# A planned instruction order: other prices for its engines and transfers, spaced products in the running bank, and four more buffers

## The chip, the cores and the metric

The kernel runs on one core of one Trainium2 chip. The time is that of the device in microseconds (us). Three runs of the kernel before gave 995.69, 995.76 and 1001.08 us; the median is 995.76 us. The profile is of one further execution.

## The reference

Attention over 4 batches, 8 heads, 576 tokens and head size 64, four heads with a local mask and four with a strided one; then, on 2304 tokens of 512 features, a gated unit with 1536 hidden features and a softplus unit with 2048:

```python
scores = np.where(masks[None], scale * q @ k.T, -1e9)      # per batch and head
attn = softmax(scores);  x = (attn @ v) laid out as (2304, 512)
xn = x / np.sqrt(np.mean(x * x, -1) + 1e-6) * rms_g
x = (silu(xn @ w_gate) * (xn @ w_val)) @ w_out
h = x @ w_in
out = (np.maximum(h, 0) + np.log1p(np.exp(-np.abs(h)))) @ w_out2
```

The weights come as 64-bit floats, and the kernel reads their bit patterns.

## The kernel before

**Stages.** Attention comes first: 4 batches of 4 head pairs, each pair cut in two, which makes 32 units, numbered 0 to 31 here. A unit has score products (L442), a softmax on VectorE and ScalarE (L454 to L469), transposes (L486), value products (L510) and a copy into `xs`. The queries and keys of a pair have two buffers for each kind of mask, so loads run at most four pairs ahead. When the first 512 tokens are through, their statistics (L347 to L354), their normalisation (L363) and their first gated products are run among the later units; so too for the next 512. Then comes the gated unit for the first 1024 tokens (side 0) and for the other 1280 (side 1), then the softplus unit for side 0 and side 1. A side has two chunks of 512 tokens; side 1 has an odd chunk of 256 as well.

**Products.** Each 32-bit operand is split into a high and a low half (ScalarE rounds, VectorE or GpSimd subtracts), and three products stand for one (`mm3`, L327). Side 0 of the gated unit multiplies plainly (`plain`, L596). The other sides use seven block products for eight (`quad`, L609): one bank, `a`, keeps a running sum. It takes a product, ScalarE copies it out (L619), and only then may it take the next one; so with every product in `a` after the first. Between two of them stands whatever `fill()` puts there (a call of `drain`): one output product (`out1`, `out2`) of an earlier hidden block out of the list `todo`. A second bank, `f`, is read by an add (`plus`, L623) and started afresh in the next `quad`. The products of the odd chunk stand behind the `quad`.

**Weights.** `decode` (L262) loads 512 KB of 64-bit weights into one of two `raw` tiles, makes 32-bit values on ScalarE (L269) and VectorE (L270 to L275), and writes 256 KB to the DRAM tensor `w_kept`, from which `fetch` (L281) reads them later. In side 1 of the gated unit the weights of the softplus unit are decoded ahead, three blocks for each hidden block (`early2`), through the two `cvt` tiles; a `cvt` tile is free when its write to `w_kept` has landed.

**Order.** The whole program is recorded as nodes (`Program.add`) with an engine, a duration and what they read and write. `emit` (L76) then runs a list schedule with these durations: on each engine the node that is ready and due first; due times come from TensorE's own order. A transfer occupies the queue (SP) for 650 ns and its result is ready 1800 ns + 6 ns per KB later, whatever else is under way. TensorE has two lists, the main one and the side one for what is run among the units (`fill`, L806), and takes the head that can begin earlier; within a list its order is that of the program. The order that comes out is fixed: each engine runs its own queue in order, and the waits are semaphores.

## Time and profile before

| | before |
|---|---|
| median of the runs | 995.76 us |
| the profiled execution | 997.98 us |
| its span | 996.2 us |
| TensorE busy | 913.8 us (92%) |
| VectorE busy | 731.4 us (73%) |
| ScalarE busy | 462.2 us (46%) |
| GpSimd busy | 208.9 us (21%) |

The span is the profiled execution without 1.78 us around it. The busy time of TensorE is modelled and overlaps from one product to the next: 222 products of 512 columns in a stretch of 50 us are a full engine. A row of a wait names the instruction that waited and the one that released it.

### The profile page before, as it was taken

What the parts mean: (1) busy time and instruction counts of PE and PEld (TensorE: products, weight loads), DVE (VectorE), ACT (ScalarE), POOL (GpSimd) and SP (SyncE); (2) the same over time, 40 slices, a digit from 0 to 9 for tenths busy, and PEclk for the clock granted to TensorE, in tenths of its full rate; (3) what the DMA queues carried; (4) which work ended last, traced back from release to release, by engine and by line L of the source; (5) the groups of instructions that cost most, each with busy time, mean ns of one, the idle gap of its engine ahead of it and who ended that gap; (6) DMA issues with size and microseconds to landing.
All of it is one profiled execution on the core that took longest, in us unless ns stands there. A gap on an engine that the chain in (4) does not pass through costs nothing.

```text
span 996.2 us, 14061 instructions
## 1 busy us (share of the span) xinstructions
PE 913.8 (92%) x5244; PEld 756.1 (76%) x5244; DVE 731.4 (73%) x1234; ACT 462.2 (46%) x867; POOL 208.9 (21%) x181
## 2 busy tenths in 40 slices
PE   6667869999999889999999988999998899999998
PEld 5556657888888667887787876888886688888877
DVE  6658638899867878688788888767779666666644
ACT  4557664444434344444444454545555444444430
POOL 2335555000013523323333252000004000000000
PEclk9876789999999989999999999999999999999999
DMA  9996112666640345244544202211220401111002
GB/s 198 240 214 164 49 59 95 215 203 216 191 133 14 101 141 180 86 143 148 183 130 148 64 12 64 64 43 43 64 64 12 137 22 43 43 43 42 22 1 106
DMA packets 42036, 103.12 MB, mean 104 GB/s; under 512 B 5040, under 2 KB 5744, under 8 KB 41968
## 3 DMA queue, kind: packets, MB, share of 16 engines
q1 hardware_dynamic: 41968, 102.23, 35.7%
q8 instruction: 41, 0.67, 0.3%
q14 instruction: 27, 0.22, 0.1%
HBM read 79.66 MB, written 22.54 MB: 103 GB/s over the span
## 4 chain that ended last, share of the span: by engine, by line
PE 67%; DVE 15%; DMA 10%; ACT 4%; issue 3%; POOL 1%; SPq 0%; DVEq 0%; ACTq 0%; POOLq 0%
PE bank L333 64%; DMA raw<-w 3%; DMA w_kept<-cvtx 3%; DVE xs L255 2%; DVE w L255 2%; DMA vb<-v_loc 2%; DVE cvu L272 2%; DVE xs L700 1%; DMA rg_sb<-rms_g 1%; DVE win L255 1%; PE bank L510 1%; PE bank L442 1%; DMA ql<-q_t 1%; DVE cvu L270 1%; DVE wout L255 1%
## 5 line engine op out<-in xcount | busy, mean ns | idle before, releaser
L333 PE MATMUL bank<-ob,win 128*128 128x512 f32 (+1 forms) x1560 | 327.4, 360 | 3.0 <-POOL ob L257 1.8
L333 PEld LDWEIGHTS bank<-ob,win 128*128 128x128 f32 x1560 | 264.4, 191 | 48.4 <-POOL ob L257 2.6
L333 PE MATMUL bank<-tb,win 128*128 128x512 f32 x672 | 178.0, 401 | 28.7 <-ACT gv L619 23.6
L333 PEld LDWEIGHTS bank<-tb,win 128*128 128x128 f32 x672 | 126.9, 192 | 64.1 <-ACT gv L619 30.7
L304 ACT ACTIVATE win<-w 128x512 fp32r<-128x512 f32 (+1 forms) x136 | 83.8, 616 | 93.7 <-DVE w L255 32.1
L718 DVE TENSOR_TENSOR xs<-bank,xs 128x512 f32<-128x512 f32 x126 | 86.3, 686 | 36.3 <-PE bank L333 35.9
L255 DVE TENSOR_TENSOR win<-w,win 128x512 fp32r<-128x512 f32 x112 | 83.6, 746 | 23.2 <-ACT win L304 21.1
L333 PE MATMUL bank<-wout,ghx 128*128 128x512 f32 x304 | 93.8, 389 | 0.2 <-DVE xs L718 0.2
L333 PE MATMUL bank<-gh,wout 128*128 128x512 f32 (+1 forms) x256 | 83.7, 355 | 3.0 <-DVE xs L700 1.7
L333 PE MATMUL bank<-ghx,wout 128*128 128x512 f32 x224 | 84.4, 392 | 1.9 <-DVE gvx L671 1.9
L333 PE MATMUL bank<-wout,gh 128*128 128x512 f32 x272 | 84.2, 390 | 0.7 <-DVE xs L718 0.7
L257 POOL TENSOR_TENSOR win<-w,win 128x512 fp32r<-128x512 f32 x24 | 40.5, 1696 | 164.2 <-ACT win L304 149.2
L700 DVE TENSOR_TENSOR xs<-bank,xs 128x512 f32<-128x512 f32 (+1 forms) x100 | 62.2, 628 | 6.9 <-PE bank L333 6.4
L333 PEld LDWEIGHTS bank<-wout,ghx 128*128 128x128 f32 x304 | 57.0, 188 | 12.5 <-issue 0.6
L333 PEld LDWEIGHTS bank<-wout,gh 128*128 128x128 f32 x272 | 50.5, 188 | 11.6 <-DVE xs L718 1.6
L333 PE MATMUL bank<-wout,glx 128*128 128x512 f32 x152 | 59.2, 389 | 0.0
L255 DVE TENSOR_TENSOR w<-w 128x256 f32<-128x256 f32 x112 | 56.7, 507 | 1.5
L272 DVE SCALAR_TENSOR_TENSOR cvu<-raw,cvu 128x512 uint32<-128x512 uint32 x68 | 56.6, 833 | 1.6
L333 PEld LDWEIGHTS bank<-gh,wout 128*128 128x128 f32 x256 | 46.4, 190 | 12.9 <-DVE xs L700 4.9
L623 DVE TENSOR_TENSOR gv<-bank,gv 128x512 f32<-128x512 f32 x44 | 30.3, 689 | 35.1 <-PE bank L333 19.1
L333 PE MATMUL bank<-wout,gl 128*128 128x512 f32 x136 | 52.9, 389 | 0.0
L333 PEld LDWEIGHTS bank<-ghx,wout 128*128 128x128 f32 x224 | 42.3, 189 | 10.9 <-DVE gvx L671 2.1
(119 smaller groups left out, 1365.9 us busy)
## 6 DMA issues: line engine op xcount, KB each, us to landing
raw<-w SPq DMA_DIRECT2D x68, 512.0 KB, 4.2
w<-w_kept SPq DMA_DIRECT2D x56, 256.0 KB, 2.8
w_kept<-cvtx SPq DMA_DIRECT2D x27, 256.0 KB, 3.9
cvt<-w_kept SPq DMA_DIRECT2D x27, 256.0 KB, 2.7
w_kept<-w SPq DMA_DIRECT2D x24, 256.0 KB, 4.0
out<-xs SPq DMA_DIRECT2D x18, 256.0 KB, 2.0
w_kept<-cvt SPq DMA_DIRECT2D x17, 256.0 KB, 4.0
cvtx<-w_kept SPq DMA_DIRECT2D x17, 256.0 KB, 2.9
```

Source lines behind the costliest of these rows:

```text
L255: dve(n, lambda: getattr(nc.vector, name)(o, x, y), r, w)
L257: pool(n, lambda: getattr(nc.gpsimd, name)(o, x, y), r, w)
L270: dve(512, lambda: nc.vector.tensor_scalar(out=u, in0=t.bitcast(U32), scalar1=0x80000000, scalar2=None, op0=ALU.bitwise_and), [kt], [ku], ...
L272: dve(512, lambda: nc.vector.scalar_tensor_tensor(out=u, in0=wlo, scalar=29, in1=u, op0=ALU.logical_shift_right, op1=ALU.bitwise_or), [kra ...
L304: act(n, lambda: nc.scalar.activation(h, t, AF.Copy), [kt], [reg(0, o + lo, o + hi)])
L333: lambda a=a, b=b, i=i, st=st, mv=mv: nc.tensor.matmul(o, lhsT=st[a], rhs=mv[b], start=(first and i == 0), stop=(last and i == m - 1), ski ...
L442: pr.add("PE", 108 if loc else 81, lambda a=a, h=h: nc.tensor.matmul(sp[64 * h:64 * h + 64, a * nk:(a + 1) * nk], lhsT=qt[:, h, q0 + a * s ...
L510: pr.add("PE", 81, lambda a=a, h=h, o=o, t=t: nc.tensor.matmul(xb[64 * h:64 * h + 64, a * nq:(a + 1) * nq], lhsT=vt[r0:r1, v0 + a, 64 * h: ...
L623: dve(CH, lambda: nc.vector.tensor_add(o[0], y[0], o[0]), [y[1], o[1]], [o[1]])
L700: dve(n, lambda: nc.vector.tensor_add(x, pb, x), [kp, kx], [kx])
L718: dve(DM, lambda: nc.vector.tensor_add(x, pb, x), [kp, kx], [kx])
```

## The change

The planner's prices change: a fixed part of 110 instead of 69 ns for VectorE, 100 ns + n/0.98 instead of 93 ns + n/1.2 for ScalarE, 2.5 instead of 2.2 ns per element for GpSimd. Transfers now share one rate: each lands 5 ns per KB after the one before it has landed or after its own issue + 400 ns, whichever is later, and is ready 1100 ns after that. The due time of what feeds a transfer counts 10 ns per KB. `quad` takes a function of the place, `gap(k)`: in both units of side 1 the two products of the odd chunk stand in gaps 1 and 2 between products of the running bank, gap 0 is empty, and gaps hold one or two output products. What is read by the softplus out of a bank goes into four halves of the `raw` tiles (`spare`) and no longer into the `gv` ring.

```diff
@@ -54,8 +54,9 @@
         self.nodes, self.seen, self.ends = [], {}, []
         self.free = dict.fromkeys(HOP, 0.0)
         self.side = False
-
-    def add(self, eng, dur, fn, r=(), w=(), lag=0):
+        self.landed = 0.0
+
+    def add(self, eng, dur, fn, r=(), w=(), kb=0):
         i = len(self.nodes)
         deps = set()
         for (key, lo, hi), wr in [(x, False) for x in r] + [(x, True) for x in w]:
@@ -71,7 +72,7 @@
             keep.append((lo, hi, i, wr))
             self.seen[key] = keep
         deps.discard(i)
-        self.nodes.append((eng, dur, fn, deps, lag, self.side))
+        self.nodes.append((eng, dur, fn, deps, 5 * kb, self.side))
 
     def emit(self, start=5000):
         nodes, n0, n = self.nodes, len(self.ends), len(self.nodes)
@@ -101,7 +102,7 @@
                 t += nodes[i][1]
         for i in reversed(new):
             for j in succ[i]:
-                due[i] = min(due[i], due[j] - nodes[i][1] - nodes[i][4] - HOP[nodes[i][0]])
+                due[i] = min(due[i], due[j] - nodes[i][1] - nodes[i][4] * 2 - HOP[nodes[i][0]])
         streams = [[i for i in new if nodes[i][0] == "PE" and nodes[i][5] == s] for s in (False, True)]
         heads = [0, 0]
         free = self.free
@@ -143,7 +144,10 @@
                 _, i = heapq.heappop(avail[e])
             begin[i] = at
             free[e] = at + nodes[i][1]
-            ends[i] = free[e] + nodes[i][4]
+            ends[i] = free[e]
+            if e == "SP":
+                self.landed = max(self.landed, at + 400) + nodes[i][4]
+                ends[i] = self.landed + 1100
             for j in succ[i]:
                 ready[j] = max(ready[j], ends[i] + hop(i, j))
                 left[j] -= 1
@@ -178,16 +182,16 @@
         return (key, 0, 1 << 30)
 
     def dve(n, fn, r, w, fast=False):
-        pr.add("DVE", 69 + n / (1.92 if fast else 0.96), fn, r, w)
+        pr.add("DVE", 110 + n / (1.92 if fast else 0.96), fn, r, w)
 
     def act(n, fn, r, w, table=False):
-        pr.add("ACT", 93 + n / 1.2, fn, r + ([all_of("table")] if table else []), w)
+        pr.add("ACT", 100 + n / 0.98, fn, r + ([all_of("table")] if table else []), w)
 
     def pool(n, fn, r, w):
-        pr.add("POOL", 110 + n * 2.2, fn, r, w)
+        pr.add("POOL", 110 + n * 2.5, fn, r, w)
 
     def dma(kb, fn, r, w):
-        pr.add("SP", 650, fn, r, w, lag=1800 + 6 * kb)
+        pr.add("SP", 650, fn, r, w, kb=kb)
 
     def table(name):
         pr.add("ACT", 1300, lambda: nc.scalar.preload_act_table_set(name), [], [all_of("table")])
@@ -606,7 +610,7 @@
         prod(bank, i, terms, n)
         return bank[0][:, :n], bank[1]
 
-    def quad(i, fill):
+    def quad(i, gap):
 
 
         a, (x, f) = a_banks.next(), x_banks
@@ -627,16 +631,16 @@
         prod(f, i, term(S1, T1))
         prod(x, i, term(A12, B21))
         plus(p1, x)
-        fill()
+        gap(0)
         prod(a, i, term(S2, T2), first=False)
         u2 = copy(a)
-        fill()
+        gap(1)
         prod(a, i, term(S3, T3), first=False)
         u3 = copy(a)
         plus(u3, f)
-        fill()
+        gap(2)
         prod(a, i, term(A22, T4), first=False)
-        fill()
+        gap(3)
         prod(f, i, term(S4, B22), first=False)
         plus(u2, f)
         return (p1, a), (u2, u3)
@@ -671,10 +675,14 @@
         dve(n, lambda: nc.vector.tensor_mul(a, vb_, a), [kv, ka], [ka])
         return halves(a, ka, n, eng, r4)
 
+    spare = [(r.bitcast(F32)[:, x * 512:(x + 1) * 512], (f"raw{i}", x << 19, (x + 1) << 19))
+             for i, r in enumerate(raws.t) for x in (0, 1)]
+
     def chain2(src, n=CH, r4=False):
         h, kp = src
         if "bank" in kp[0]:
-            l, kl = fk["gv"].next()
+            l, kl = spare.pop(0)
+            spare.append((l, kl))
         else:
             l, kl = h, kp
         l, h = l[:, :n], h[:, :n]
@@ -844,22 +852,32 @@
                 build(c0, c1, c4)
             for f in range(0 if side else 1, W1N):
                 prep1(f, side, (0, 1) if side or f > 1 else (1,))
-                more = drain if f < W1N - 1 else lambda: drain(len(todo) > 3)
+                w = w_at(f, side)
                 if side:
-                    (gb0, vb0), (gb1, vb1) = quad(w_at(f, side), more)
+                    odd = []
+
+                    def gap(k):
+                        if 0 < k < 3:
+                            odd.append(plain(w, k - 1, c4, o_banks))
+                        if k == 2:
+                            g[f, c4] = chain1(*odd, 256, True)
+                        if k and (f < W1N - 1 or len(todo) > 4):
+                            drain(2 if f % 2 else 1)
+
+                    (gb0, vb0), (gb1, vb1) = quad(w, gap)
                     g[f, c0] = chain1(gb0, vb0)
                     g[f, c1] = chain1(gb1, vb1)
                     for k in range(3 * f, min(3 * f + 3, 2 * W2N)):
                         early2(k)
+                    drain(max(0, len(todo) - 6))
                 else:
                     for c in cs:
-                        gate = plain(w_at(f, side), 0, c, p_banks)
-                        more()
-                        g[f, c] = chain1(gate, plain(w_at(f, side), 1, c, p_banks), eng="DVE")
-                        more()
-                if c4 is not None:
-                    g[f, c4] = chain1(*[plain(w_at(f, side), row, c4, o_banks) for row in (0, 1)], 256, True)
-                    drain(2)
+                        gate = plain(w, 0, c, p_banks)
+                        if f < W1N - 1 or len(todo) > 3:
+                            drain(1)
+                        g[f, c] = chain1(gate, plain(w, 1, c, p_banks), eng="DVE")
+                        if f < W1N - 1 or len(todo) > 3:
+                            drain(1)
                 if f % 2:
                     drain(len(todo))
                     todo += outs1(f, f == 1, cs)
@@ -873,12 +891,15 @@
             n2 = W2N // 2
             for p in range(n2):
                 i = prep2(p, c4 is not None)
-                (x0, y0), (x1, y1) = quad(i, drain if p < n2 - 1 else lambda: None)
+                def gap(k):
+                    if c4 is not None and 0 < k < 3:
+                        g[2 * p + k - 1, c4] = chain2(plain(i, k - 1, c4, o_banks), 256, True)
+                    elif k and p < n2 - 1:
+                        drain(2)
+
+                (x0, y0), (x1, y1) = quad(i, gap)
                 for f, c, x in ((2 * p, c0, x0), (2 * p + 1, c0, y0), (2 * p, c1, x1), (2 * p + 1, c1, y1)):
                     g[f, c] = chain2(x)
-                if c4 is not None:
-                    for row in (0, 1):
-                        g[2 * p + row, c4] = chain2(plain(i, row, c4, o_banks), 256, True)
                 drain(len(todo))
                 todo += [(out2, [2 * p, 2 * p + 1], g, p == 0, c, j, p == n2 - 1)
                          for c in cs for j in range((CUTS[c + 1] - CUTS[c]) // 128)]
```

Lines of the changed kernel have other numbers (L333 is L337, L347 is L351, L442 is L446). TensorE's queue in attention, around the statistics of the first 512 tokens (`ssq,ones`; `kl,ql` and `ks,qs` are score products of one unit each, `pt,vb` value products, `id_sb` transposes). Before, they stand behind unit 18:

```order
L486 MATMUL bank_73<-id_sb,eb_110 96x128
L442 MATMUL bank_70<-ks_102,qs_98 64x54 x12
L347 MATMUL bank_76<-ssq,ones 128x512
L510 MATMUL bank_75<-pt_114,vb_104 64x64 x6
L510 MATMUL bank_75<-pt_115,vb_104 64x64 x2
```

Changed, they stand behind unit 13, and the first gated product behind unit 14:

```order
L446 MATMUL bank_71<-kl_101,ql_97 64x96 x8
L351 MATMUL bank_76<-ssq,ones 128x512
L514 MATMUL bank_74<-pt_114,vb_105 64x64 x6
L514 MATMUL bank_74<-pt_115,vb_105 64x64 x4
L490 MATMUL bank_72<-id_sb,eb_111 96x128 x3
L490 MATMUL bank_73<-id_sb,eb_111 96x128
L446 MATMUL bank_70<-ks_103,qs_99 64x54 x12
L337 MATMUL bank_77<-ob,win_89 128x512
```

The side work of the first chunk has moved five units ahead. TensorE's queue in side 1 of the gated unit, the first `quad` (bank_70 is the running bank, `tb,win` its products two to four, bank_73 is `f`, 128x256 the odd chunk). Before:

```order
L333 MATMUL bank_70<-ob,win_89 128x512 x6
L333 MATMUL bank_73<-tb,win_89 128x512 x6
L333 MATMUL bank_72<-ob,win_89 128x512 x6
L333 MATMUL bank_70<-tb,win_89 128x512 x18
L333 MATMUL bank_73<-ob,win_89 128x512 x6
L333 MATMUL bank_74<-ob,win_89 128x256 x12
L333 MATMUL bank_75<-ob,win_89 128x256 x12
```

Changed:

```order
L337 MATMUL bank_70<-ob,win_89 128x512 x6
L337 MATMUL bank_73<-tb,win_89 128x512 x6
L337 MATMUL bank_72<-ob,win_89 128x512 x6
L337 MATMUL bank_70<-tb,win_89 128x512 x6
L337 MATMUL bank_74<-ob,win_89 128x256 x12
L337 MATMUL bank_70<-tb,win_89 128x512 x6
L337 MATMUL bank_75<-ob,win_89 128x256 x12
L337 MATMUL bank_70<-tb,win_89 128x512 x6
L337 MATMUL bank_73<-ob,win_89 128x512 x6
```

The odd chunk's products now part the three groups of six. The same queue at the end of an odd hidden block (f = 3; bank_73 is `f`, bank_70 the next running bank). Before, output products and the odd chunk stand between the last product in `f` and its next start:

```order
L333 MATMUL bank_77<-gh_1530,wout_1517 128x256
L333 MATMUL bank_77<-gl_1533,wout_1517 128x256
L333 MATMUL bank_77<-gh_1530,wout_1517 128x256
L333 MATMUL bank_70<-ob,win_89 128x512 x6
L333 MATMUL bank_73<-tb,win_89 128x512 x6
L333 MATMUL bank_72<-ob,win_89 128x512 x6
```

Changed:

```order
L337 MATMUL bank_77<-gl_1533,wout_1517 128x256
L337 MATMUL bank_77<-gh_1530,wout_1517 128x256
L337 MATMUL bank_71<-tb,win_1516 128x512 x6
L337 MATMUL bank_73<-ob,win_1516 128x512 x6
L337 MATMUL bank_70<-ob,win_89 128x512 x6
L337 MATMUL bank_73<-tb,win_89 128x512 x6
L337 MATMUL bank_72<-ob,win_89 128x512 x6
```

Between the last product in `f` (bank_73<-ob) and its next start (bank_73<-tb) one group of six is left.

## Rows read from the trace of the kernel before

**Rows 1.** Stretch, length, busy (count) PE, PEld, DVE, ACT, POOL; PEclk, DMA share, GB/s.

```profile
0.00:150.00 150.00, 105.97 (x1475) 87.32 (x1476) 93.71 (x214) 86.73 (x201) 66.13 (x79) 0.80 0.67 154
150.00:312.00 162.00, 161.01 (x703) 132.79 (x702) 134.49 (x218) 69.26 (x117) 20.18 (x16) 0.99 0.54 164
340.00:356.00 16.00, 9.72 (x31) 7.03 (x30) 7.09 (x12) 4.69 (x8) 0.00 (x0) 0.75 0.56 181
356.00:606.00 250.00, 232.16 (x1183) 194.06 (x1181) 203.77 (x317) 112.64 (x204) 88.00 (x64) 0.99 0.37 117
789.00:991.00 202.00, 200.63 (x973) 169.29 (x973) 126.23 (x208) 83.19 (x151) 0.00 (x0) 1.00 0.11 36
```

**Rows 2.** Two stretches of attention, columns as above.

```profile
50.00:75.00 25.00, 16.83 (x267) 14.06 (x267) 13.97 (x36) 12.29 (x36) 8.41 (x11) 0.77 1.04 214
75.00:100.00 25.00, 19.84 (x288) 16.04 (x289) 22.55 (x42) 18.28 (x45) 14.61 (x16) 0.66 0.69 164
```

**Rows 3.** Timeline of the DMA queue: start, us, issue.

```profile
81.03 0.34 SPq L429 DMA_DIRECT2D vb<-v_loc  x1
89.29 0.48 SPq L420 DMA_DIRECT2D kl<-k_loc  x1
...
94.70 0.59 SPq L420 DMA_DIRECT2D ks<-k_str  x1
```

**Rows 4.** Timeline of VectorE, the first chunk's normalisation.

```profile
81.95 3.67 DVE L255 TENSOR_TENSOR xs<-xs,ssq 128x512 f32<-128x512 f32 x4
```

**Rows 5.** Timeline of TensorE: unit 13, first statistics, unit 30, the gated unit's start.

```profile
47.55 1.48 PE L442 MATMUL bank<-kl,ql 128*64 128x96 f32 x16
...
69.84 1.12 PE L347 MATMUL bank<-ssq,ones 128*128 128x512 f32 x2
...
123.86 0.91 PE L442 MATMUL bank<-ks,qs 128*64 128x54 f32 x24
...
150.36 12.75 PE L333 MATMUL bank<-ob,win 128*128 128x512 f32 x48
```

**Rows 6.** TensorE's waits at 350:585, then at 745:790: us, times, longest.

```profile
PE bank L333 <- ACT gv L619: 20.3, 15, 5.6
...
PE bank L333 <- ACT gv L619: 3.3, 2, 2.6
PE bank L333 <- ACT gvx L619: 1.8, 2, 1.2
```

**Rows 7.** Timeline of TensorE, running bank, side 1; in brackets the wait before.

```profile
342.48 1.52 PE L333 MATMUL bank<-tb,win 128*128 128x512 f32 x6
349.58 2.92 PE L333 MATMUL bank<-tb,win 128*128 128x512 f32 x6 [5.59 <-ACT gv L619]
353.20 2.93 PE L333 MATMUL bank<-tb,win 128*128 128x512 f32 x6 [0.69 <-ACT gv L619]
...
497.43 1.65 PE L333 MATMUL bank<-tb,win 128*128 128x512 f32 x6 [0.63 <-ACT gv L619]
```

**Rows 8.** Timeline of ScalarE in the same stage.

```profile
413.21 0.66 ACT L269 ACTIVATE cvtx<-raw 128x512 f32<-128x512 f32 x1 [3.45 <-DMA w_kept<-cvtx]
413.77 0.58 ACT L619 ACTIVATE gv<-bank 128x512 f32<-128x512 f32 x1
```

**Rows 9.** The page's DMA issues: count, KB each, us to landing.

```profile
w<-w_kept SPq DMA_DIRECT2D x56, 256.0 KB, 2.8
w_kept<-cvtx SPq DMA_DIRECT2D x27, 256.0 KB, 3.9
...
out<-xs SPq DMA_DIRECT2D x18, 256.0 KB, 2.0
```

**Rows 10.** A full stretch (columns as Rows 1), then groups: busy, mean ns, idle.

```profile
250.00:300.00 50.00, 50.00 (x222) 41.43 (x221) 38.38 (x63) 19.07 (x33) 2.58 (x2) 1.00 0.57 168
...
L333 PE MATMUL bank<-ob,win 128*128 128x256 f32 x480 | 60.7, 283 | 0.0
...
L623 DVE TENSOR_TENSOR gv<-bank,gv 128x512 f32<-128x512 f32 x44 | 30.3, 689 | 35.1 <-PE bank L333 19.1 <-ACT gv L619 15.6
```

## The prediction, made before the change was run

> **What bounds the kernel now.** I read the stages first, then TensorE's waits, then the engine that releases each wait. The stages [rows 1] show three kinds of time. From 150 to 312 us and from 789 to 991 us TensorE is busy for 161.0 of 162 us and 200.6 of 202 us: nothing is left there, and 222 products of 512 columns in 50 us [rows 10] make 0.225 us for one; one of 256 columns takes 60.7 / 480 = 0.126 us. From 340 to 606 us (side 1 of the gated unit) it is idle for 6.3 + 17.8 = 24.1 us. The first 150 us (attention) are of another kind: no engine is full, and the transfers are full in the first part only.
>
> In attention the reader is to see the handing over of the bound. From 50 to 75 us the DMA engines are full at 214 GB/s; from 75 to 100 us their share is 0.69 at 164 GB/s, while VectorE is busy for 22.6 of 25 us [rows 2]. Between 81.03 and 89.29 us nothing is issued [rows 3], because VectorE runs the normalisation of the first chunk (3.67 us for its four products alone [rows 4]) in front of the softmax that would free the buffers. The last keys are issued at 94.70 us [rows 3], and their score products (unit 30) run at 123.86 us [rows 5]: the units lag by 29 us when the transfers are through.
>
> In side 1 of the gated unit 20.3 of the idle us are waits of the running bank for ScalarE's copy, 15 of them [rows 6]. Two sorts stand there [rows 7]: the bare round trip (0.69 us with nothing between two groups, 0.63 us behind an output product of 256 columns) and a copy that is late. Why it is late, ScalarE's queue shows [rows 8]: a weight conversion waits 3.45 us for the `w_kept` write that frees its tile, and the copy that TensorE needs stands right behind.
>
> **The change, part by part.** The sum is made against the profiled execution, 997.98 us; the median of the runs, 995.76, lies 2.22 us below it, and the forecast is moved by as much.
>
> *No arithmetic.* No product, copy or transfer is added or removed. After attention TensorE has one list, so its order there changes only where the code says so; the new prices move the other four queues. Where TensorE is full today (150 to 312 and 789 to 991 us [rows 1]) I cost this at nothing, because its own backlog covers it; if a queue falls behind there, the cover goes at the rate of the wait.
>
> *Prices in attention.* The statistics of the first chunk move from behind unit 18 to behind unit 13; the trace had these at 69.84 and 47.55 us [rows 5], so the side work comes some 22 us earlier, into the stretch where the transfers are full and VectorE is busy for only 14.0 of 25 us [rows 2]. Loads run four pairs ahead, so that a VectorE burst there need not empty the DMA queue. The hole it made is worth 25 x (1 - 164/214) = 5.8 us [rows 2]. The two first weight blocks, loaded four loads earlier, only change places with loads of queries: the bytes are the same. The second chunk's burst moves too (unit 26 to unit 23), which takes part of the 29 us of lag away; I take 4 us of it. Bounds: nothing shown excludes that a burst at unit 13 tears a hole of its own, so +6; at best the lag goes down by 22, which with the hole makes -28. I take **-10**, nearer to the hole, which a row shows, than to the lag, which is work that has to be done somewhere: VectorE's 93.7 us of attention [rows 1] do not shrink.
>
> *Products spaced apart.* In gaps 1 and 2 each copy gets 12 products of 256 columns as cover, 12 x 0.126 = 1.5 us, with output products besides. Before, it had nothing in the first two blocks, 6 x 0.225 = 1.35 us behind an output product of 512 columns and 6 x 0.126 = 0.76 us behind one of 256. The short waits [rows 7] go, since 0.69 us was the whole of the round trip's overhang. The longest wait, 5.6 us [rows 6], keeps 4.1 behind a cover of 1.5. The other 14 have 14.7 us, 1.05 on average and so mostly under the cover; I leave 2.4 us for those above it. So 20.3 - 4.1 - 2.4 = 13.8: **-14**. Bounds: after the wait of 5.59 us the next two groups of six took 2.92 and 2.93 us instead of 1.52 [rows 7], at a granted clock of 0.75 on average over 340 to 356 us [rows 1], the lower level (1.2 GHz) for part of it. If that wait goes, 2 x 1.4 = 2.8 us more come back: at best -23. At worst only the bare round trips go; I take six of the 15 for such, 4 us.
>
> A rule speaks on the late ones. The rows show a write to `w_kept` landing after 3.9 us and a read of the same size after 2.8, but the writes of the output, of the same 256 KB, after 2.0 [rows 9]: writing is not slow, the `w_kept` writes stand behind 512 KB loads. The new shared rate says so too (a lone 256 KB transfer 0.4 + 1.3 + 1.1 = 2.8 us, more behind another), where the old price was 3.99 us whatever was under way. The Trainium skill (DMA: Bandwidth & Descriptors, on where the fixed 2 us go) holds that the receipt of a write is most of it and heaviest for DRAM. By that page a write should be dearer than a read, and the plan, which prices both alike, would set the conversions too early; the term would be -4 in place of -14. The output rows speak against it.
>
> *The odd block's end.* Behind an odd block nothing stands any more between the last product in `f` and its next start but one group of six, 1.35 us. VectorE's add there takes 0.69 us [rows 10] and VectorE is busy for 203.8 of 250 us [rows 1], so one instruction of that size ahead of it is likely: 1.38 us and two handings over against 1.35. I take 0.4 us for each of five such ends: **+2**. Bounds: 0, and two more instructions ahead each time, 5 x 1.4 = +7. What waits behind it is the whole of TensorE.
>
> *Last stage and other buffers.* The first `quad` of the softplus unit's side 1 waits 3.3 + 1.8 = 5.1 us for copies [rows 6]; two of its gaps now have 1.5 us of cover: **-3** (bounds -5 and 0). The `spare` buffers leave the `gv` ring to three copies per `quad`; the stage shows no wait for that ring while TensorE is full, so nothing more.
>
> **Sum.** -10 - 14 + 2 - 3 = -25; 997.98 - 25 = 973, and 2.2 lower, 971 us. Its own range is 956 to 985.
>
> **Rivals.**
> - *The lag of the units goes as well.* If the softmax follows the loads once both bursts lie early, attention gains 28 instead of 10: 953 us. For it: the 29 us between [rows 3, 5], VectorE's idle time before 75 us [rows 2]. Against: 93.7 us of VectorE's work in chains that cross four engines.
> - *The order does not do what it says.* The late copies stay, and attention keeps its hole at another place: only -4 and -3 remain, 995.8 - 7 = 989 us, within 1%. The Trainium skill's rule on writes, above, would lead here too. For it: TensorE's queue is in order, and a plan that is off by a microsecond waits all the same. Against: the cover of 1.5 us does not depend on the plan.
> - *A new wait takes over, slower.* Single gated products now stand between the units on TensorE, in front of value products. If the normalisation of the first chunk is not ready when its first product's turn comes, TensorE, the softmax behind it and the buffers stop, and a second hole opens: +6; with the `f` bank at its worst, +7, and the spacing at no more than -1 (the two 0.69 us): 995.8 + 12 = 1008 us. It decides if transfers run faster than planned, so that unit 14 is there before the burst at unit 13 is over. Against: 214 GB/s [rows 2] is near the plan's 1024 / 5 = 205, and the cover in the gaps.
>
> **How the numbers follow.** 0.57 for the forecast, 0.20, 0.15 and 0.08 for the rivals in their order. A measurement of this kernel can tell about 1%, or 10 us: below 985.8 us is faster, above 1005.7 slower. Faster takes the first two, 0.77; the same 0.15; slower 0.08. The range leaves out the last rival, a third of the first at its low end and a third of the second at its high end, together 0.08 + 0.07 + 0.05 = 0.20: 948 to 994 us.
>
> **What would show it.** Right: the first statistics on TensorE near 50 us and no hole in the DMA queue around 81 us; the gated unit's 48 products starting near 140 instead of 150.36 us; waits for the copy in side 1 below 8 us in all, none of the 0.6 to 0.7 sort; full clock at its start. Wrong: waits of `f`-bank products for the add above 5 us in all; conversions still waiting for `w_kept` ahead of a copy, with TensorE idle; a stretch of attention in which both DMA and VectorE stand idle; and, for the sum as a whole, new idle time in the two stages that are full today, where I cost the other queues' new order at nothing.

## The result, and the profile after

The changed kernel takes 951.22 us (median of 4 runs, 949.16 to 952.55), the kernel before 995.73 us beside it (4 runs, 991.11 to 1001.08): a ratio of 0.9549, interval 0.9498 to 0.9600. That is 44.5 us less, where 25 were forecast; 951 lies in the range, near its low end. The profiled execution took 952.55 us, its span is 950.7 us.

First where the time went. The stages are cut at four places that every version has: the gated unit's 48 products after the last statistics, and the first product of the kind `tb,win` (the second `quad` operand) in each of the three stages that use it. The last stage ends with the start of the last product; 4.2 us of the span follow it. One profiled execution each, in us:

| stage | before | after | difference | forecast |
|---|---|---|---|---|
| attention, up to the 48 products | 150.4 | 126.5 | -23.8 | -10 |
| gated unit, side 0 | 189.4 | 188.7 | -0.7 | 0 |
| gated unit, side 1 | 268.5 | 254.2 | -14.3 | -14 + 2 |
| softplus unit, side 0 | 170.0 | 169.8 | -0.2 | 0 |
| softplus unit, side 1 | 213.7 | 207.3 | -6.4 | -3 |

In the changed kernel's windows (columns as in Rows 1) the first, second and last stretch answer to [rows 1]; side 1 of the gated unit is cut in three.

```profile
0.00:126.00 126.00, 99.53 (x1474) 80.36 (x1475) 92.79 (x214) 87.12 (x201) 62.88 (x79) 0.83 0.76 183
126.00:288.00 162.00, 161.34 (x705) 132.78 (x704) 135.08 (x218) 69.95 (x117) 20.77 (x16) 0.99 0.54 164
313.80:329.80 16.00, 15.93 (x81) 13.21 (x81) 11.79 (x21) 8.25 (x15) 2.12 (x2) 1.00 0.48 151
329.80:543.00 213.20, 205.00 (x1063) 174.02 (x1062) 184.77 (x285) 98.48 (x179) 64.57 (x51) 0.99 0.45 141
543.00:567.00 24.00, 18.28 (x82) 14.32 (x82) 23.90 (x30) 11.94 (x21) 16.16 (x11) 0.96 0.11 33
748.00:946.00 198.00, 197.75 (x950) 166.64 (x949) 125.42 (x206) 78.28 (x148) 0.00 (x0) 1.00 0.12 37
```

Three things are to be seen. VectorE does the same work in attention (92.8 us against 93.7) in 24 us less. The start of side 1 is full at a granted clock of 1.00, the upper level (2.4 GHz), where it was 9.7 of 16 us at 0.75. And the end of side 1 is a new hole: 18.3 of 24 us.

Attention in stretches of 25 us; the second and third answer to [rows 2]:

```profile
25.00:50.00 25.00, 17.94 (x271) 15.40 (x271) 19.85 (x48) 15.29 (x36) 12.65 (x15) 0.72 1.03 237
50.00:75.00 25.00, 22.34 (x300) 17.21 (x301) 22.12 (x49) 17.58 (x47) 13.65 (x17) 0.73 1.01 228
75.00:100.00 25.00, 21.19 (x316) 16.41 (x314) 20.31 (x42) 19.66 (x43) 13.34 (x15) 0.93 0.57 139
100.00:125.00 25.00, 21.31 (x378) 16.97 (x375) 14.60 (x39) 22.11 (x51) 16.87 (x21) 1.00 0.28 93
```

From 50 to 75 us the transfers are as full as before (1.01) and now VectorE is busy beside them, for 22.1 us where it was 14.0 [rows 2]. The DMA queue's timeline (start, us, issue) still has a hole at 81 us. Nothing is issued from 81.17 to 87.77, which is 6.6 us where it was 8.3 [rows 3]; two loads more are through by then:

```profile
78.17 0.33 SPq L282 DMA_DIRECT2D w_kept<-w  x1
79.15 0.33 SPq L433 DMA_DIRECT2D vb<-v_loc  x1
80.64 0.48 SPq L424 DMA_DIRECT2D kl<-k_loc  x1
81.17 0.59 SPq L422 DMA_DIRECT2D ql<-q_t  x1
87.77 0.35 SPq L433 DMA_DIRECT2D vb<-v_str  x1
...
89.21 0.60 SPq L424 DMA_DIRECT2D ks<-k_str  x1
```

The next load waits there for value products that free a `vb` buffer. On TensorE these stand behind the statistics of the second chunk, which wait for GpSimd:

```profile
82.84 1.13 PE L351 MATMUL bank<-ssq,ones 128*128 128x512 f32 x2 [2.24 <-POOL ssq L554]
```

TensorE's timeline (first statistics, first gated product, unit 30, the gated unit's start) answers to [rows 5]:

```profile
50.08 2.08 PE L351 MATMUL bank<-ssq,ones 128*128 128x512 f32 x2 [2.19 <-POOL ssq L554]
...
58.49 0.79 PE L337 MATMUL bank<-ob,win 128*128 128x512 f32 x1 [2.58 <-ACT ob L254]
...
109.79 0.91 PE L446 MATMUL bank<-ks,qs 128*64 128x54 f32 x24
...
126.54 12.09 PE L337 MATMUL bank<-ob,win 128*128 128x512 f32 x48
```

The last keys are issued 5.5 us earlier (89.21 against 94.70); their products follow 20.6 us behind instead of 29.2; and the rest of attention behind them takes 16.8 us instead of 26.5. So 5.5 + 8.6 + 9.7 = 23.8. Seen from TensorE, its idle time in attention falls from 44.0 to 26.5 us, and its products take 99.5 instead of 106.0 us, at a mean granted clock of 0.83 instead of 0.80. The two waits in brackets, 2.2 and 2.6 us, are part of what the early side work costs at its new place: in front of all statistics and gated products of attention TensorE waits 11.1 us, where it waited 5.4.

TensorE's waits in side 1, 314 to 567 us (us in total, times, longest), answer to the first row of [rows 6]:

```profile
PE bank L337 <- ACT gv L623: 5.3, 5, 1.8
PE bank L337 <- DVE xs L708: 3.3, 2, 2.6
PE bank L337 <- DVE gvx L675: 1.9, 3, 1.1
PE bank L337 <- POOL gl L261: 1.7, 1, 1.7
PE bank L337 <- POOL glx L261: 0.6, 1, 0.6
PE bank L337 <- DVE gv L627: 0.5, 2, 0.3
PE bank L337 <- ACT gvx L623: 0.4, 1, 0.4
```

ScalarE's waits of the same stretch, for the conversions of [rows 8]:

```profile
ACT cvtx L273 <- DMA w_kept<-cvtx: 3.5, 5, 1.1
```

The copy waits are 5.7 us instead of 20.3, and the conversions wait 3.5 us for `w_kept`. The wait for the add into `f` (`gv L627`) is 0.5 us. New are 5.6 us for `xs`, `gl` and `glx`, all at the end, where VectorE is busy for 23.9 of 24 us. In the last stage, at 705 to 750 us, the copy waits of [rows 6] are 2.1 us instead of 5.1:

```profile
PE bank L337 <- ACT gv L623: 1.4, 1, 1.4
PE bank L337 <- ACT gvx L623: 0.7, 1, 0.7
```

### The profile page after: what moved, and what is told of

The parts are those of the page before. It is cut to its first block, busy times and chain, and to the rows that moved or that the text cites. A ratio compares the mean times of both kernels' runs of the same rounds, so it can differ in the third digit from the quotient of the medians.

```text
span 950.7 us, 13991 instructions
## 1 busy us (share of the span) xinstructions
PE 901.4 (95%) x5244; PEld 747.5 (79%) x5244; DVE 739.1 (78%) x1234; ACT 458.2 (48%) x867; POOL 200.1 (21%) x181
## 4 chain that ended last, share of the span: by engine, by line
PE 68%; DVE 18%; DMA 6%; issue 3%; ACT 3%; POOL 1%; SPq 1%; DVEq 0%; ACTq 0%
PE bank L337 63%; DVE w L259 3%; PE bank L446 2%; DMA w_kept<-cvtx 2%; PE bank L514 2%; DVE xs L259 2%; DVE xs L708 2%; DMA w<-w_kept 1%; DMA vb<-v_loc 1%; DVE cvu L276 1%; PE bank L490 1%; DMA ql<-q_t 1%; DVE win L259 1%; DVE cvtx L279 1%; DVE gv L627 1%
## 5 line engine op out<-in xcount | busy, mean ns | idle before, releaser
L337 PE MATMUL bank<-ob,win 128*128 128x512 f32 (+1 forms) x1560 | 330.3, 359 | 4.2 <-ACT ob L254 2.6
L337 PEld LDWEIGHTS bank<-ob,win 128*128 128x128 f32 x1560 | 267.4, 191 | 50.9 <-ACT ob L254 2.8
L337 PE MATMUL bank<-tb,win 128*128 128x512 f32 x672 | 173.5, 394 | 9.9 <-ACT gv L623 6.7
L337 PEld LDWEIGHTS bank<-tb,win 128*128 128x128 f32 x672 | 124.0, 188 | 40.3 <-ACT gv L623 9.7
L337 PE MATMUL bank<-wout,ghx 128*128 128x512 f32 x304 | 94.1, 391 | 0.6 <-DVE xs L726 0.6
L259 DVE TENSOR_TENSOR win<-w,win 128x512 fp32r<-128x512 f32 (+1 forms) x112 | 79.3, 709 | 17.8 <-ACT win L308 17.5
L337 PE MATMUL bank<-gh,wout 128*128 128x512 f32 (+1 forms) x256 | 82.8, 357 | 5.9 <-DVE xs L708 3.3
L337 PE MATMUL bank<-wout,gh 128*128 128x512 f32 x272 | 84.0, 390 | 0.0
L337 PE MATMUL bank<-ghx,wout 128*128 128x512 f32 x224 | 83.5, 390 | 0.1
L708 DVE TENSOR_TENSOR xs<-bank,xs 128x512 f32<-128x512 f32 (+1 forms) x100 | 62.2, 630 | 15.5 <-PE bank L337 14.3
L261 POOL TENSOR_TENSOR win<-w,win 128x512 fp32r<-128x512 f32 x24 | 37.3, 1555 | 166.4 <-ACT win L308 149.3
L259 DVE TENSOR_TENSOR w<-w 128x256 f32<-128x256 f32 x112 | 68.2, 609 | 1.4
L337 PEld LDWEIGHTS bank<-wout,ghx 128*128 128x128 f32 x304 | 56.6, 188 | 13.2 <-DVE xs L726 1.9
L337 PE MATMUL bank<-wout,glx 128*128 128x512 f32 x152 | 59.3, 390 | 0.3 <-DVE glx L259 0.3
L337 PEld LDWEIGHTS bank<-wout,gh 128*128 128x128 f32 x272 | 50.8, 188 | 10.8 <-DVE xs L726 0.4
L337 PEld LDWEIGHTS bank<-gh,wout 128*128 128x128 f32 x256 | 46.6, 192 | 14.0 <-DVE xs L708 3.7
L337 PE MATMUL bank<-wout,gl 128*128 128x512 f32 x136 | 52.9, 389 | 0.0
L276 DVE SCALAR_TENSOR_TENSOR cvu<-raw,cvu 128x512 uint32<-128x512 uint32 x68 | 49.5, 728 | 1.3
L337 PEld LDWEIGHTS bank<-ghx,wout 128*128 128x128 f32 x224 | 42.1, 188 | 9.0 <-DVE wout L259 0.5
L663 ACT ACTIVATE gh<-gvx 128x512 fp32r<-128x512 f32 (+1 forms) x38 | 21.2, 559 | 57.0 <-PE bank L337 41.3
```

What stands on the lines that cost most here:

```text
L259: dve(n, lambda: getattr(nc.vector, name)(o, x, y), r, w)
L261: pool(n, lambda: getattr(nc.gpsimd, name)(o, x, y), r, w)
L276: dve(512, lambda: nc.vector.scalar_tensor_tensor(out=u, in0=wlo, scalar=29, in1=u, op0=ALU.logical_shift_right, op1=ALU.bitwise_or), [kra ...
L337: lambda a=a, b=b, i=i, st=st, mv=mv: nc.tensor.matmul(o, lhsT=st[a], rhs=mv[b], start=(first and i == 0), stop=(last and i == m - 1), ski ...
L663: act(n, lambda: nc.scalar.activation(h, src, AF.Copy), [ksrc], [kh])
L708: dve(n, lambda: nc.vector.tensor_add(x, pb, x), [kp, kx], [kx])
```

## The experiments

The table gives each kernel's median and extremes, its ratio to the kernel before in the same batch with the 95% interval, and the lengths of the five stages in its profiled execution. The kernel before had medians of 1000.09 us (19 runs), 999.64 (7) and 999.36 (17) in these batches.

| kernel | median us (extremes) | ratio (interval) | attention | side 0 | side 1 | softplus 0 | softplus 1 |
|---|---|---|---|---|---|---|---|
| before | see above | 1 | 150.4 | 189.4 | 268.5 | 170.0 | 213.7 |
| the change | 951.22 (949.16-952.55) | 0.9549 (0.9498-0.9600) | 126.5 | 188.7 | 254.2 | 169.8 | 207.3 |
| e1, all prices alone | 947.69 (947.04-949.81) | 0.9488 (0.9426-0.9549) | 125.2 | 188.8 | 245.4 | 167.9 | 214.8 |
| e2, spacing alone | 1000.81 (995.05-1001.86) | 1.0012 (0.9978-1.0046) | 150.4 | 189.4 | 275.3 | 169.9 | 210.1 |
| e3, buffers alone | 999.67 (992.57-1001.75) | 0.9992 (0.9953-1.0031) | 151.1 | 189.4 | 273.1 | 171.6 | 210.5 |
| e4, change without buffers | 951.13 (949.48-953.87) | 0.9528 (0.9453-0.9602) | 125.5 | 189.1 | 251.7 | 168.4 | 208.7 |
| e5, transfer rate alone | 961.16 (959.88-967.48) | 0.9637 (0.9587-0.9687) | 129.3 | 189.5 | 252.7 | 172.4 | 210.6 |
| e6, engine prices alone | 984.31 (981.01-994.15) | 0.9898 (0.9830-0.9965) | 147.3 | 188.1 | 262.1 | 167.7 | 215.1 |
| e7, spacing in the last stage only | 945.03 (944.32-947.76) | 0.9471 (0.9423-0.9518) | 125.1 | 188.7 | 247.3 | 170.3 | 207.3 |
| e8, outputs placed as before | 946.02 (943.68-946.50) | 0.9468 (0.9429-0.9507) | 125.2 | 189.1 | 249.1 | 169.7 | 207.3 |
| e9, late side work | 964.24 (963.62-964.88) | 0.9655 (0.9617-0.9694) | 142.7 | 188.7 | 247.1 | 167.8 | 211.9 |
| e10, third conversion tile | 992.81 (989.12-999.39) | 0.9967 (0.9936-0.9999) | 149.8 | 189.9 | 267.3 | 170.4 | 210.5 |
| e11, last block as before | 947.35 (945.95-949.43) | 0.9512 (0.9480-0.9544) | 124.8 | 188.9 | 248.6 | 170.3 | 207.3 |

A stage of a single execution must be read with care. In side 1 of the gated unit every engine has the same order in the kernel before and in e3, and still the one took 268.5 and the other 273.1 us; in the last stage the kernel before and e5 differ in the place of a single VectorE instruction, and they took 213.7 and 210.6 us. TensorE's idle time and the time of its products tell the two parts apart (us, from the windows of these stages):

| | before | e3 | e2 | e1 | the change | e11 | e5 |
|---|---|---|---|---|---|---|---|
| side 1: idle | 24.1 | 23.5 | 26.4 | 8.2 | 14.0 | 9.4 | |
| side 1: products, granted clock | 244.3, 0.97 | 249.7, 0.95 | 248.9, 0.95 | 237.2, 1.00 | 240.3, 0.99 | 239.2, 0.99 | |
| last stage: idle | 4.7 | 2.8 | | 4.3 | 0.3 | | 2.8 |
| last stage: products, granted clock | 209.0, 0.99 | 207.7, 1.00 | | 210.5, 0.98 | 207.1, 1.00 | | 207.8, 1.00 |

**One part alone: e1, e2, e3.** e1 keeps the hunks of the diff in `Program`, `dve`, `act`, `pool` and `dma`; e2 those in `quad` and the two `gap` functions; e3 the one in `chain2`. In e2 and e4 a `quad` of the softplus unit's side 1 asks the ring of four `gv` tiles for a fifth, which is the first again, while that one still holds the sum `p1` that the softplus reads behind the `quad`. That value is lost there, so these two runs stand for the time of an order and not for a whole result.

```diff
 e1   self.landed = max(self.landed, at + 400) + nodes[i][4]
 e1   ends[i] = self.landed + 1100
 e2   gap(k): odd.append(plain(w, k - 1, c4, o_banks)) ...
 e3   l, kl = spare.pop(0); spare.append((l, kl))
```

> The kernel before with the new planner prices alone (transfers and engines), the old fill and the old gv ring. Theory (each part pays in its own stage): attention ends at about 127 us instead of 150, side 1 of the gated unit stays within 5 us of the old 268, the last stage within 2 us of the old 215; about 971 us in all. Rival (the prices do all of it, the gaps are incidental): side 1 about 254, the last stage about 209, about 952 us. Rival (the parts need each other): attention gains under 10 us here.

> The kernel before with the new gaps alone: the odd chunk's products and the output products between the products of the running bank, old prices, old gv ring. Theory (each part pays in its own stage): attention unchanged at 150 us, side 1 of the gated unit about 256 us instead of 268, the last stage 210 to 213 instead of 215; about 980 us. Rival (the prices do all of it): side 1 within 4 us of 268, about 994 us.

> The kernel before with the four further buffers for the softplus values alone. Theory: the last two stages change by less than 1 us each, since these waited for no buffer of that ring; 995 us. Rival (the ring held the copies back): the last stage 2 to 4 us shorter, 992 us.

e1 is as fast as the whole change or faster; e2 and e3 are within 0.5% of the kernel before. Of the 44.5 us the prices give all: the first rival of e1 (254 us in side 1, 952 in all) is met or bettered, but not in the last stage (214.8 us, where it named 209). In e2 both the theory (256 us in side 1) and the rival (within 4 us of 268, 994 in all) miss; the theory of e3 holds for the whole as far as its spread of 9 us can tell. Its last stage is 3.2 us shorter, as its rival named, but e5 and e10 have 210.6 and 210.5 us there without the buffers. The waits of side 1 say how: TensorE's waits and ScalarE's for `w_kept`. First e2 (338 to 613 us), with spacing and old prices:

```profile
ACT cvtx L269 <- DMA w_kept<-cvtx: 18.4, 6, 5.2
...
PE bank L333 <- ACT gvx L619: 10.4, 3, 4.6
...
PE bank L333 <- ACT gv L619: 8.5, 7, 4.7
```

Then e1 (313 to 558 us), with the old fill and new prices; TensorE's waits, ScalarE's, and three of the seven waits of the running bank on TensorE's timeline:

```profile
PE bank L337 <- ACT gv L623: 5.7, 7, 1.9
PE bank L337 <- DVE xs L704: 2.4, 4, 1.1
```

```profile
ACT cvtx L273 <- DMA w_kept<-cvtx: 2.8, 6, 0.8
```

```profile
319.04 1.65 PE L337 MATMUL bank<-tb,win 128*128 128x512 f32 x6 [0.75 <-ACT gv L623]
...
321.38 1.65 PE L337 MATMUL bank<-tb,win 128*128 128x512 f32 x6 [0.69 <-ACT gv L623]
...
337.07 1.65 PE L337 MATMUL bank<-tb,win 128*128 128x512 f32 x6 [1.95 <-ACT gv L623]
```

With the cover and the old prices waits of 4.6 and 4.7 us for late copies stay, 18.9 us in all: 1.5 us of products do not cover a copy that is so late. With the prices and no cover they are gone: six of the seven waits left are 0.33 to 0.75 us, about a bare round trip or less, and only one is longer. The row of the kernel before for the conversions (338 to 607 us) is

```profile
ACT cvtx L269 <- DMA w_kept<-cvtx: 28.1, 11, 4.7
```

28.1 us with old prices, 18.4 with the spacing, 2.8 with new prices alone. My reading of side 1 before these runs, that the cover gives its 14 us, fell here.

These conversions are not the whole cause of the late copies. Followed back in the trace of the kernel before, from the copy over at most 12 us, five of the 15 waits (9.9 of 20.3 us) lead to a conversion that waited for `w_kept`; three are bare round trips (2.0 us); six (6.2 us) lead through VectorE's queue, with weight work in it; and in one (2.2 us) other work of ScalarE stood in front of the copy. In e2 the three waits for `gvx` (10.4 us) stand behind the rounding of a weight that waited for VectorE. The one of 4.56 us, on ScalarE's timeline:

```profile
488.90 0.63 ACT L304 ACTIVATE win<-w 128x512 fp32r<-128x512 f32 x1 [2.58 <-DVE w L255]
489.43 0.58 ACT L619 ACTIVATE gvx<-bank 128x512 f32<-128x512 f32 x1
```

So what the new prices mend is the place of the weight work in both queues; no run parts the two.

**Two parts together, and the two kinds of price: e4, e5, e6.** e4 is the change without `spare`; e5 has the shared transfer rate alone, e6 the three engine prices alone.

```diff
 e5   "SP" nodes as changed; 69 + n/0.96, 93 + n/1.2, 110 + 2.2 n kept
 e6   110 + n/0.96, 100 + n/0.98, 110 + 2.5 n; lag=1800 + 6 * kb kept
```

> The changed kernel without the four further buffers (the softplus values in the gv ring again). Theory: within 1 us of the changed kernel, 951 us. Rival (with the odd chunk's values now asked for inside the quad, the ring of four runs out): the last stage 3 to 6 us longer, 955 us.

> The kernel before with the shared transfer rate alone; prices of VectorE, ScalarE and GpSimd as before. Theory (the planner saw transfers that it did not have, and this is the whole of the gain): attention ends near 126 us, side 1 of the gated unit takes 245 to 249 us, 948 us in all, as with all prices. Rival (the dearer ScalarE and VectorE place the copies in side 1): attention 126, but side 1 258 or more, 960 us.

> The kernel before with the three prices of the engines alone (fixed parts and rates of VectorE, ScalarE, GpSimd); transfers priced as before, no spaced products, no other buffers. The shared transfer rate alone gave 129.3 us for attention and 252.7 for side 1 of the gated unit (before: 150.4 and 268.5). Theory (the rate is what counts, since the engine prices leave the statistics behind units 18 and 25): attention 147 to 151, side 1 260 to 269, the whole 985 to 1000 us. Rival (each set of prices alone does most of it, because any truer price moves the conversions away from the copies): attention below 140, side 1 below 256, the whole below 975.

The four buffers take no time and give none; they are what makes the spaced order of the last stage possible without a clash. e5 falls between its theory and its rival: the whole is the rival's 960 us, side 1 with 252.7 us neither's. The transfer rate gives the larger part, and the two kinds of price nearly add up: in attention -21.1 and -3.1 make -24.2 (e1: -25.1), in side 1 of the gated unit -15.8 and -6.4 make -22.2 (e1: -23.1). TensorE's waits for copies in side 1 are 8.0 us in e5 and 16.2 in e6. e6 keeps to its theory in attention and side 1 (147.3 in 147 to 151, 262.1 in 260 to 269) and leaves it in the whole by 0.7 us (984.3 against 985); the engine prices are worth some 10 us, the interval of the ratio being 0.983 to 0.9965. The rate also sets the place of the statistics. On TensorE's timeline of e5 the first stand at 48.53 us:

```profile
48.53 1.82 PE L351 MATMUL bank<-ssq,ones 128*128 128x512 f32 x2 [0.87 <-POOL ssq L554]
```

In e6 they stand behind unit 18 as before, at 63.97 us.

**How much of attention is the early side work: e9.** e1, with the side list held back so that the first statistics come behind unit 20 and the second behind unit 29.

```diff
+ if x and heads[0] < len(streams[0]) and streams[0][heads[0]] < streams[1][heads[1]]:
+     continue
- START = (16, 21, 29, 36, 36)
+ START = (18, 24, 29, 36, 36)
```

> All new prices, old fill, but the side work of the first two chunks is held back on TensorE until the units recorded ahead of it are through (first statistics behind unit 20, second behind 29, where the old order had 18 and 25). Theory (attention is shorter since the side work lies in the stretch where transfers are full): attention ends at 145 us or later, 965 us or more. Rival (the new order of the loads does it): attention at 131 us or less, 951 us.

On TensorE's timeline the first statistics of e9 are at 71.54 us, 1.7 us later than those of the kernel before [rows 5]:

```profile
71.54 1.12 PE L353 MATMUL bank<-ssq,ones 128*128 128x512 f32 x2
```

Attention takes 142.7 us, 2.3 short of the theory's 145 and far from the rival's 131. So of e1's 25.1 us the place of the side work gives 17.5, and 7.7 come without it, from the order of the loads and the other queues. The 17.5 us are an upper value: the second statistics stand four units later in e9 than in the kernel before, at 106.49 instead of 103.84 us.

**Is it the buffer that the conversions wait for: e10.** The kernel before with a third tile for conversions, in a part of `ssq_b` that nothing reads any more; TensorE's and GpSimd's orders are unchanged.

```diff
- cvt.t.append(wb.tile([128, 512], F32, name="cvtx"))
+ cvt.t += [wb.tile([128, 512], F32, name="cvtx"), ssq_b[:, :512]]
```

> The kernel before with a third tile for the conversions (the first 512 columns of the ssq_b tile, which nothing reads after the last normalisation); old prices, old fill; TensorE's and GpSimd's orders are those of the kernel before, word for word. Theory (TensorE's late copies in side 1 come from conversions that wait in ScalarE's queue for the w_kept write: 28.1 us there, 20.3 us of running-bank waits): the waits of conversions for w_kept fall below 8 us, those of the running bank below 10, side 1 goes from 268.5 to 250 to 258, attention stays at 150, the whole 980 to 989 us. Rival (the queue order itself is wrong and the conversion waits for the next thing, its load or the shared cvu tile): running-bank waits stay above 15 us, side 1 264 to 270, the whole 993 to 1001.

The rival holds: side 1 takes 267.3 us (the whole, 992.81, is 0.2 us below the rival's 993). ScalarE's waits there, of e10 (338 to 607 us):

```profile
ACT cvt L269 <- DMA w_kept<-cvt: 13.9, 3, 8.0
...
ACT cvtx L269 <- DMA raw<-w: 5.5, 2, 4.0
ACT ssq_b L269 <- DMA w_kept<-ssq_b: 4.7, 2, 2.8
ACT cvtx L269 <- DMA w_kept<-cvtx: 3.2, 2, 1.6
...
ACT ssq_b L269 <- DMA raw<-w: 2.1, 1, 2.1
ACT cvt L269 <- DMA raw<-w: 2.1, 1, 2.1
```

The conversions wait 21.8 us for `w_kept` and 9.7 us for their loads, 31.5 us in all where it was 28.1. A buffer more does not help an order that expects the transfers too early: the planner uses it to put the conversion earlier still, and it then waits for the next transfer. The longest late copy of e10, 5.0 us, leads back to such a load. The wait of copies stays at 18.1 us (17.4 and 0.7). The whole is 0.33% faster, at the edge of what the interval can tell.

**What the spacing costs in side 1 of the gated unit: e7, e8, e11.** At new prices side 1 grows by the spacing from 245.4 to 254.2 us (e9 and e7, with e1's order there: 247.1 and 247.3; e4, with the change's order: 251.7). At old prices, 268.5 and 275.3 us, 2.3 us of the difference are idle time of TensorE and the rest lies within what one order differs by. e7 has everything but the gated unit's spacing; e8 the odd chunk in gaps 1 and 2 but the output products as before, one in each gap and two behind the `quad`; e11 is the change with the odd chunk of the last hidden block alone behind the `quad`.

```diff
 e7   quad(w, lambda k: more())
 e8   gap(k): odd chunk in gaps 1, 2; more()   # and drain(2) behind the quad
 e11  - if 0 < k < 3:
 e11  + if 0 < k < 3 and f < W1N - 1:
```

> All new prices and the four buffers; the odd chunk in the gaps in the softplus unit only, the gated unit with the old fill. Theory (the gaps cost in the gated unit and pay in the softplus unit): side 1 of the gated unit 245 us as with the prices alone, the last stage 208 us, 941 us in all. Rival (either stage depends on how the other leaves the queues): no better than 947.

> The changed kernel, but in the gated unit the output products stand where they stood before (one in each of the four gaps, two behind the quad); the odd chunk stays in gaps 1 and 2. Theory (what costs in side 1 is that nothing covers the end of an odd block and the stage's end): side 1 at 246 to 248 us, 943 us. Rival (the place of the odd chunk itself costs, since it no longer stands behind the quad): side 1 at 252 or more, 950 us.

> The whole change, except that in the last hidden block of the gated unit's side 1 the odd chunk's products stand behind the quad, as before, in place of gaps 1 and 2. Theory (what the spacing costs in side 1 is the uncovered chain at its end: waits for gl, glx and xs of 1.7, 0.6 and 3.3 us, and a clock that falls there to 0.93): side 1 from 254.2 to 248 to 251, the whole 945 to 948 us. Rival (the cost is spread over all blocks, by outputs bunched in gaps 1 to 3 and an empty gap 0): 253 to 255 and 950 to 952 us.

The timeline of the changed kernel shows where: the last output products of side 1 stand right behind the `quad`, and their operands are not there yet.

```profile
546.52 0.50 PE L337 MATMUL bank<-gh,wout 128*128 128x512 f32 x1
548.74 0.50 PE L337 MATMUL bank<-gl,wout 128*128 128x512 f32 x1 [1.72 <-POOL gl L261]
...
555.06 0.50 PE L337 MATMUL bank<-glx,wout 128*128 128x512 f32 x1 [0.60 <-POOL glx L261]
...
563.20 0.38 PE L337 MATMUL bank<-gh,wout 128*128 128x256 f32 x1 [2.60 <-DVE xs L708]
```

Before, the odd chunk's 24 products, 24 x 0.126 = 3.0 us, stood there and covered the last `gl` chain. e11 puts them back in this one block, and its window over the same end reads

```profile
538.00:562.00 24.00, 22.43 (x126) 18.24 (x125) 23.10 (x33) 11.35 (x21) 16.48 (x11) 1.00 0.00 1
```

22.4 of 24 us instead of 18.3, at a granted clock of 1.00 instead of 0.96, and side 1 takes 248.6 us instead of 254.2. TensorE's idle time in side 1, 8.2 us in e1, is 14.0 in the change and 9.4 in e11. So 4.6 of the 5.8 idle us by which the change stands above e1 are the uncovered end of one block, and e11's theory holds; the medians of the whole, 951.22 and 947.35 us, differ by 3.9. e8 gets 5.1 us of side 1 back too with the `gl` wait of 1.7 us still there, so the two mends overlap; its side 1, 249.1 us, is a little above its theory (246 to 248). The remaining 2 to 3 us (e7 247.3, e11 248.6, e1 245.4) are within what single executions differ by, and I leave them open.

e7 is the fastest, though neither at its theory's 941 nor at its rival's 947: 945.03 us, ratio 0.9471, all its runs (944.32 to 947.76) below all of the change's (949.16 to 952.55), although not measured in the same batch. e8 beside it, at 946.02, can't be told from it.

## Why the prediction was right, and which steps of it were not

**Direction and range** hold: faster by 4.5%, 951 in 948 to 994. The size is that of the first rival, 953 us, not of the forecast of 971.

**Prices in attention, -10: mis-sized, -23.8 measured.** The side work moves into the stretch in which VectorE had room, as named, and the first statistics came at 50.08 us as said. Two things failed. The hole in the DMA queue did not go: 6.6 us of it stay at the same time, now in part behind TensorE's wait for the second chunk's statistics and no longer behind VectorE's normalisation. It gives 1.7 of the 5.5 us by which the last keys are issued earlier, so that these come near the 5.8 us set down for it is luck. And the choice between the bounds failed: I took the hole and left the lag, because VectorE's 93.7 us "do not shrink". They did not (92.8). But VectorE was idle for 11.0 of 25 us at 50 to 75 us [rows 2], and work that moves there no longer stands in front of the softmax at the end; e9, which puts it back, loses 17.5 us. The lag fell by 8.6 us and the tail behind unit 30 by 9.7; the bound of -28 was the nearer one. The first rival's chance of 0.20 was too low.

**Products spaced apart, -14: right in size, wrong in kind.** Side 1 lost 14.3 us, the copy waits fell below 8 us (one bare round trip of 0.66 us is left) and the clock at its start was full, as forecast. But e2 has the spacing without the prices and gains nothing there (its idle time is 26.4 us against 24.1), and e1 has the prices without it and gains 23.1; that the sum of a gain from the prices and a loss from the spacing comes to 14 is luck. The failed step is "the other 14 ... mostly under the cover": the late copies came from weight work that stood in front of them, conversions held for a transfer in 9.9 of the 20.3 us and VectorE's queue in another 6.2, and they went when the order placed that work otherwise. The rows before showed one such copy and how late its write lands [rows 8, 9], and I counted it only as a risk to the spacing.

**The rule on writes.** The writes to `w_kept` land no sooner than before (4.2 us after, 3.9 in [rows 9]; the output's still 2.0), yet a plan with one price for reads and writes brought the conversions' waits for them from 28.1 us to 3.5. The Trainium skill (DMA: Bandwidth & Descriptors, on where the fixed 2 us go) would have had this plan set the conversions too early, with a term of -4; the trace disagrees. What delays these writes here is what was queued before them: in the trace of the changed kernel the five of the 27 `w_kept<-cvtx` writes that were issued with nothing else under way landed after 1.99 to 2.03 us, the other 22 after up to 5.4, while reads of 256 KB that were alone from issue to landing took 2.5 to 2.7. The page's row after:

```profile
w_kept<-cvtx SPq DMA_DIRECT2D x27, 256.0 KB, 4.2
```

**The odd block's end, +2.** The wait for the add was 0.5 us in all, so the term was too dear. The uncovered chain was at another place that I did not look for: the end of the last hidden block, 5.6 us. The step that failed is that a move out of a place was costed only between two `quad`s, not where no next `quad` follows.

**Last stage, -3: -6.4 measured**, beyond the bound of -5. 4.4 us of it are idle time (4.7 to 0.3), within the bound; the other 2 are products at a granted clock of 1.00 instead of 0.99, and e5, with TensorE's old order, had that clock too. Here it is the spacing: the four executions with the change's order in this stage (the change, e7, e8, e11) took 207.3 us each, and the seven with TensorE's old order (the kernel before, e1, e3, e5, e6, e9, e10) 210.5 to 215.1. e2's -3.6 at old prices shows nothing, since e3 and e10 have -3.2 without the spacing.

**Edits at nothing** held: side 0 of either unit moved by 0.7 us at most, and the buffers cost nothing (e3, e4). Neither the second nor the third rival occurred as a whole. The third one's mechanism is there in small: TensorE waits at the new places of the side work (11.1 us in attention instead of 5.4), and one hole in the queue stands behind such a wait; the gain of 23.8 us is what is left after it.

## What to carry to other kernels

Where a static order is made from prices, the price that lets queued transfers overlap freely is the first to mend: here it put weight work in front of copies that an in-order queue could not pass, and one shared rate was worth 3.6 of the 5.1% that all prices gave. Look at what heads the queue of the engine that is late, not only at the wait of the engine that bounds: more cover (e2) and more buffers (e10) left TensorE's waits for copies at 18.9 and 18.1 us of 20.3. And when work is moved out of a loop's tail to give cover elsewhere, ask what it covered in the last round.

## What was not expected of the hardware

Executions of one order differ by an amount that depends on the order. The kernel before ran in 991.05 to 1004.92 us in 18 of the 19 runs of one batch, e3 and e10, with the old prices, in 992.57 to 1001.75 (10 runs) and 989.12 to 999.39 (12 runs). The orders made with all new prices spread over 1.3 us (e9) to 4.4 us (e4), with 4 to 6 runs each; e5, with the rate alone, over 7.6 us (4 runs).

One pair of traces shows what varies in one stage. In side 1 the kernel before and e3 have the same order in every engine, and TensorE's waits for copies are 20.3 and 20.7 us, its idle time 24.1 and 23.5. Its products took 244.3 and 249.7 us, at granted clocks of 0.97 and 0.95. So there it was the granted clock and not the waits. Whether this holds for the other stages and runs is not shown.
